# Cross attention and gated FFN on one core: loads placed in the list of steps, a new order of the steps, and a new order of the last products

## The chip, the cores and the metric

The kernel runs on one NeuronCore of a Trainium2 chip. What counts is the device time of one execution in microseconds (us); the figure given for a kernel is the median of its runs. The engines are TensorE (PE, its weight loads PEld), VectorE (DVE), ScalarE (ACT), GpSimd (POOL) and SyncE (SP); SP, ACT and POOL can issue DMAs.

## What is computed

There are 64 heads (8 batches b, 8 heads h) with 512 tokens x and 32 state rows each, of width 64. Tokens attend to the state rows, and state rows to the tokens, each without further projections. All 8 heads of a row are put side by side (width 512), and the rows, 512 + 32 per batch or 4352 in all, go through a gated FFN of inner width 1536.

```python
scores = scale * x @ state.T            # [512, 32] per head
xread  = softmax(scores) @ state        # tokens read the states
sread  = softmax(scores.T) @ x          # states read the tokens
rows   = concat([xread, sread], axis=2) # per batch 544 rows of 8*64
out    = (relu(rows @ w_gate) * (rows @ w_val)) @ w_out
```

## The kernel before, in words

**Attention and the first two FFN products in one.** As `xread` is a product with `state`, the kernel multiplies `state` with the weights first: U[b] = state[b] @ [w_gate, w_val] (steps `c` and `u`, line 299: many small matmuls, 64 rows by 32 columns; `co` and `uo` copy the result out of PSUM). A batch then needs, for each of 12 groups jf of 128 inner columns, four matmuls of 512 tokens (`ga` and `gb`, line 324): U's columns times the normalized scores of the batch, transposed (ANS). `re` (ScalarE, line 351) takes the relu of the gate half, `mu` (VectorE, line 355) the product with the value half; the result is h.

**How a batch gets its ANS.** `xT` transposes x on TensorE (line 169), `xo` copies it out, `sc` makes the scores (line 186), `ex` the exponent (ScalarE), `nr` the sums and their reciprocals (VectorE, lines 196 and 198), `nx` the scaling (line 202; VectorE, or GpSimd with `.pool`), `aT` the transpose (line 218), `ao` the copy. Each stands twice per batch, for four heads each. From batch 3 on, DMA transposes take the place of the TensorE ones.

**Down projection.** h @ w_out is made as seven products of half-size blocks, p1 to p7, instead of eight (`oh`, line 419). It needs sums of blocks: of h (`hs`, lines 385 to 387, and `hl`, line 394, on GpSimd) and of w_out (`ws.0` to `ws.3`, line 363, on GpSimd). `oc`, `oa` and `os` copy, add and store the four result blocks. The 256 state rows of all batches come last, as a ninth, smaller batch (`gvs`, line 342; `s_step`, lines 500 to 507).

**Order.** All is laid out by hand: the instructions of an engine run in the order in which they are written. For batches 0 to 2 and part of 3 the string `program` (lines 568 to 602) gives that order, word by word: `spin.7` is seven matmuls on zeros, `xT.1.0` a call of x_T(1, 0), and so on. Behind it a loop (line 650) goes through the remaining groups at a fixed lag of 18 groups between a group and its down projection. Last, `h_sums(B)` and a list of steps (line 663) run the rest: the products of the state rows, in the order p1, p2, p6, p5, p7, p4, p3, among those of the last batch (the zeros).

**Loads.** x of batch 0 comes in three parts: heads 0 and 1 over ACT's queue, heads 2 and 3 over SP's behind the states of batches 0 and 1 (lines 525 to 527), and heads 4 to 7 over GpSimd's queue, which converts to bf16 on the way. Before the first word of `program`, GpSimd issues every other load of the first stage in one go (lines 535 to 543): two pairs of 256 columns of w_gate and w_val, x of batch 1 in two halves, four more pairs, x of batch 2, the states of batches 2 to 7, and w_out in two halves. `c.b.i` needs pair i; `stT.0.2` needs the first states. The states of batches 0 and 1 come as fp32 and are cast by `stc`.

**The last stores.** The state rows' result is kept in one tile of two row blocks t of 128 rows (four batches) by two column halves m of 256. When a row block is complete (after p4, and after p3), four DMAs of 32 rows by 512 columns store it (lines 495 to 498).

Of the kernel before, what the change touches and what calls it, by code (L numbers as in the profile page):

```python
# [16 lines left out]
def kernel(  # L17
# [91 lines left out]
    def x_dma_cast(b, parts=1):

        cast_on_load.add(b)
        xb_alloc(b)
        v = xb[b].rearrange("p (h c d) -> p h c d", h=H, c=NC)
        for i in range(parts):
# [1 line left out]
            nc.gpsimd.dma_start(out=v[:, hs], in_=x[b, hs].rearrange("h (p c) d -> p h c d", c=NC))
# [289 lines left out]
    def o_half(b, n):  # L406

        p, c = PRODUCTS[n // 2], n % 2
        a, w = {"p1": (h_block(b, 0, 0), b11), "p2": (h_block(b, 1, 0), b21), "p3": (h_block(b, 1, 0), b22),
                "p4": (h_block(b, 1, 1), t4), "p7": (h_block(b, 0, 1), b12),  # L410
                "p5": (held.get(("s", b, 1)), t1), "p6": (held.get(("s", b, 2)), t2w)}[p]
# [6 lines left out]
        for i in range(HF):
            nc.tensor.matmul(ps[:, HM * c:HM * c + HM], a[:, i, 128 * c:128 * c + 128], w[:, i],  # L419
                             start=(i == 0 and (p in ("p1", "p2", "p5") and c == 0 or p == "p5" and b == B - 1)),  # L420
                             stop=(i == HF - 1),
                             skip_group_check=True)
# [60 lines left out]
    def s_end(p):  # L483

        outr = out.rearrange("(b s) m -> b s m", s=SP)
        if p == "p1":
# [4 lines left out]
        if p in ("p1", "p6", "p7", "p4"):
            nc.scalar.copy(out=dst, in_=held["acc", B, "w", 0][:, 0:HM])
        else:
            nc.vector.tensor_tensor(out=dst, in0=held["acc", B, "z", 0][:, 0:HM], in1=dst, op=ALU.add)
        if p in ("p4", "p3"):
            for bq in range(4):
# [1 line left out]
                eng.dma_start(out=outr[t * 4 + bq, S:SP], in_=held["sr"][bq * Ns:(bq + 1) * Ns, t])
# [12 lines left out]
    nc.vector.memset(warm, 0.0)
# [64 lines left out]
    re.0.5 c.0.3 mu.0.5 ga.0.4 gb.0.4 aT.1.0 co.0.3.1.act c.1.3 ao.1.0.dve re.0.4 co.0.3.0.act co.1.3.1.act
    mu.0.4 c.0.4 ga.0.6 gb.0.6 co.0.4.1.act ga.0.7 gb.0.7 co.0.4.0.dve co.1.3.0.act nx.1.1 ga.0.9 re.0.6
    re.0.7 aT.1.1 ao.1.1.act mu.0.6 mu.0.7 gb.0.9 re.0.9 ga.0.8 gb.0.8 re.0.8 mu.0.9 mu.0.8 ga.1.0 ga.1.1
    gb.1.0 ga.1.6 re.1.0 mu.1.0 gb.1.1 gb.1.6 ga.1.3 gb.1.3 ga.1.2 stT.2.4 re.1.1 re.1.6 re.1.3 mu.1.1
    sto.2.4.0.act gb.1.2 re.1.2 ga.1.5 gb.1.5 ga.1.4 gb.1.4 ga.1.7 mu.1.3 mu.1.6 mu.1.2 hs.0.0 re.1.5 mu.1.5  # L580
    gb.1.7 re.1.7 re.1.4 oh.0.0 mu.1.7 xT.2.0 xT.2.2 c.0.5 sto.2.4.1.act xT.2.1 mu.1.4 xT.2.3 co.0.5.1.dve
    xo.2.2.dve c.1.5 xo.2.1.dve co.1.5.1.dve xo.2.0.act co.0.5.0.act co.1.5.0.act ga.0.11 gb.0.11 re.0.11
    mu.0.11 xo.2.3.act ga.0.10 gb.0.10 sc.2.0 re.0.10 mu.0.10 hs.0.1 ga.1.10 gb.1.10 ex.2.0 re.1.10 ws.0.pool
    ga.1.11 sc.2.1 ex.2.1 u.2.1.0 gb.1.11 nr.2.0 re.1.11 oh.0.1 nx.2.0 uo.2.1.0.0.act mu.1.11 aT.2.0 mu.1.10
    c.1.4 uo.2.1.0.1.act u.2.0.0 ao.2.0.act oh.0.2 oh.0.3 co.1.4.0.dve ga.1.8 nr.2.1 xc.3.0.act ws.1.pool
    hs.0.2 oc.0.1 oh.0.4 co.1.4.1.act xc.3.1.pool uo.2.0.0.0.act nx.2.1.pool ga.1.9 xt.3 oa.0.3 oh.0.6
    ws.2.pool gb.1.8 re.1.8 gb.1.9 oh.0.5 ws.3.pool re.1.9 mu.1.8 aT.2.1 hl.0 uo.2.0.0.1.act xd.4 xc.4.0.pool
    xc.4.1.pool hs.1.0 ao.2.1.act oh.0.7 hs.1.2 ga.2.0 gb.2.0 mu.1.9 ga.2.3 gb.2.3 xt.4 hs.1.1 ga.2.1 gb.2.1
    re.2.0 oc.0.5 mu.2.0 re.2.1 ga.2.2 re.2.3 gb.2.2 re.2.2 mu.2.1 oh.0.8 xd.5 u.2.1.1024 mu.2.3 u.2.0.1024
    uo.2.0.1024.0.dve uo.2.1.1024.0.act uo.2.0.1024.1.act oh.0.9 u.2.1.512 u.2.0.512 oc.0.9 oh.0.10  # L590
    uo.2.0.512.0.act uo.2.1.512.1.act sc.3.0 uo.2.1.512.0.dve ga.2.5 oa.0.9 oh.0.12 oh.0.13 uo.2.1.1024.1.act
    ga.2.4 uo.2.0.512.1.act gb.2.4 oh.0.11 re.2.4 gb.2.5 ga.2.7 oc.0.11 oh.1.0 os.0.11 mu.2.2 ex.3.0 mu.2.4
    oa.0.13 re.2.5 sc.3.1 ga.2.6 mu.2.5 nr.3.0 gb.2.6 srm.0 nx.3.0 ex.3.1 oh.1.1 srn.0 re.2.6 gb.2.7 re.2.7
    mu.2.6 nr.3.1 ga.2.8 mu.2.7 gb.2.8 re.2.8 oh.1.2 mu.2.8 u.3.0.0 uo.3.0.0.0.act u.3.0.512 uo.3.0.512.0.act
    uo.3.0.0.1.act oh.1.3 stT.4.8 u.3.1.0 uo.3.1.0.0.act nx.3.1.pool ga.2.9 aD.3 gb.2.9 sto.4.8.0.act oc.1.1
    oa.1.3 re.2.9 mu.2.9 srm.1 srn.1 sto.4.8.1.act uo.3.0.512.1.act oh.1.4 oh.1.5 oc.1.5 ga.2.10 gb.2.10
    ga.2.11 re.2.10 gb.2.11 mu.2.10 re.2.11 mu.2.11 xc.5.0.act oh.1.6 oh.1.7 u.3.1.512 u.3.1.1024 u.3.0.1024
    oh.1.8 hs.2.0 uo.3.1.0.1.dve ga.3.0 gb.3.0 uo.3.1.512.0.act uo.3.0.1024.0.act xc.5.1.pool sc.4.0 ga.3.1
    oh.1.9 hl.1 uo.3.1.1024.1.dve hs.2.1 uo.3.1.1024.0.act uo.3.1.512.1.act hs.2.2 ex.4.0 ga.3.3 gb.3.1 re.3.0
    ga.3.2 uo.3.0.1024.1.dve re.3.1 gb.3.2 mu.3.0 oc.1.9 oa.1.9 re.3.2 gb.3.3 oh.1.10 re.3.3 xt.5 mu.3.3 srm.2  # L600
# [95 lines left out]
```

## Time and profile before

| what | us |
|---|---|
| median of 3 runs | 223.88 (223.06 to 224.71) |
| the profiled execution | 224.17 |
| its span, first to last instruction or DMA | 222.1 |
| PE busy in the span | 213.4 |
| first matmul of the program that is not a spin, start | 4.98 |
| first product of the down projection, start | 35.84 |
| last matmul, start of its group of six | 217.00 |
| last store, issue | 218.45 |

In a row of the timeline stand the start, the length, the engine, the line, the operation with its tiles (out<-in) and shapes, the number of instructions taken together, and, in brackets, how long the engine stood idle before and what ended that. In a row of windows stand, behind the stretch and its length, the busy time and number of instructions of PE, PEld, DVE, ACT and POOL, the granted clock, the share of the DMA engines and GB/s. In the groups of instructions stand the busy time, the mean of one in ns, and the idle time before them. In the DMA issues stand the size and the time from issue to landing, and in the queues' rows packets, MB and share.

### The profile page before, as it was taken

What the parts mean: (1) busy time and instruction counts of PE and PEld (TensorE: products, weight loads), DVE (VectorE), ACT (ScalarE), POOL (GpSimd) and SP (SyncE); (2) the same over time, 40 slices, a digit from 0 to 9 for tenths busy, and PEclk for the clock granted to TensorE, in tenths of its full rate; (3) what the DMA queues carried; (4) which work ended last, traced back from release to release, by engine and by line L of the source; (5) the groups of instructions that cost most, each with busy time, mean ns of one, the idle gap of its engine ahead of it and who ended that gap; (6) DMA issues with size and microseconds to landing.
All of it is one profiled execution on the core that took longest, in us unless ns stands there. A gap on an engine that the chain in (4) does not pass through costs nothing.

```text
span 222.1 us, 5525 instructions
## 1 busy us (share of the span) xinstructions
PE 213.4 (96%) x2214; PEld 139.3 (63%) x2214; DVE 150.3 (68%) x263; ACT 128.7 (58%) x247; POOL 164.1 (74%) x162
## 2 busy tenths in 40 slices
PE   6879999999999999999999999999999999999992
PEld 2535445565665657656765666566656666888881
DVE  3579967855486848878787778777977485343531
ACT  2468976876757883566556655656565454322231
POOL 7946199899999996699949993996299719933210
PEclk9999999999999999999999999999999999999998
DMA  6999999039195409920298037102320121021106
GB/s 160 193 196 196 193 201 282 20 62 265 31 206 201 97 0 207 243 72 3 74 233 218 3 91 191 52 0 97 83 61 0 50 97 47 3 96 47 50 27 209
DMA packets 42361, 25.32 MB, mean 114 GB/s; under 512 B 18816, under 2 KB 41856, under 8 KB 42336
## 3 DMA queue, kind: packets, MB, share of 16 engines
q1 hardware_dynamic: 29408, 17.04, 29.4%
q0 software_dynamic: 12416, 7.41, 22.1%
q10 hardware_dynamic: 512, 0.52, 0.7%
q8 instruction: 17, 0.28, 0.5%
q14 instruction: 8, 0.07, 0.1%
HBM read 18.35 MB, written 8.91 MB: 123 GB/s over the span
## 4 chain that ended last, share of the span: by engine, by line
PE 82%; POOL 7%; ACT 4%; DVE 3%; DMA 2%; issue 1%; DVEq 0%; POOLq 0%
PE gv_ps L324 34%; PE w_ps L419 17%; PE z_ps L419 12%; PE gv_ps L342 5%; PE up L299 4%; PE sc_ps L186 2%; DMA st_f<-in_state_dram 2%; POOL s L386 2%; POOL s L385 2%; POOL h_sb L387 2%; POOL h_sb L394 2%; PE zs_ps L419 1%; ACT g_sb L351 1%; PE ws_ps L419 1%; PE xT_ps L169 1%; PE upc L299 1%
## 5 line engine op out<-in xcount | busy, mean ns | idle before, releaser
L355 DVE TENSOR_TENSOR h_sb<-gv_ps,g_sb 128x512 bf16<-128x512 f32 (+1 forms) x108 | 69.1, 657 | 42.3 <-ACT g_sb L351 31.3
L324 PE MATMUL gv_ps<-ans,U 128*128 128x512 bf16 x384 | 94.9, 379 | 0.2
L351 ACT ACTIVATE g_sb<-gv_ps 128x512 bf16<-128x512 f32 (+1 forms) x108 | 61.4, 576 | 37.3 <-PE gv_ps L324 27.5
L419 PEld LDWEIGHTS <-h_sb 128*128 128x128 bf16 x510 | 49.4, 98 | 16.4 <-issue 1.7
L324 PEld LDWEIGHTS <-U 128*128 128x128 bf16 x384 | 35.7, 98 | 31.7 <-issue 1.7
L385 POOL TENSOR_TENSOR s<-h_sb 128x512 bf16<-128x512 bf16 x24 | 27.7, 1153 | 19.3 <-DVE h_sb L355 19.3
L394 POOL TENSOR_TENSOR h_sb<-h_sb,s 128x512 bf16<-128x512 bf16 x24 | 27.0, 1152 | 7.2 <-PE z_ps L419 7.2
L429 ACT COPY o_sb<-w_ps 128x512 f32<-128x512 f32 x32 | 18.8, 587 | 18.4 <-PE w_ps L419 15.8
L386 POOL TENSOR_TENSOR s<-s,h_sb 128x512 bf16<-128x512 bf16 x24 | 28.0, 1167 | 1.9
L309 ACT CAST U<-up 128x512 bf16<-128x512 f32 x43 | 22.7, 595 | 10.0 <-PE up L299 10.0
L387 POOL TENSOR_TENSOR h_sb<-h_sb 128x512 bf16<-128x512 bf16 x24 | 28.1, 1171 | 0.0
L419 PE MATMUL w_ps<-wo_sb,h_sb 128*128 128x256 bf16 x192 | 26.2, 273 | 0.0
L419 PE MATMUL z_ps<-wo_sb,h_sb 128*128 128x256 bf16 x186 | 24.1, 273 | 0.0
L419 PEld LDWEIGHTS <-s 128*128 128x128 bf16 x204 | 19.2, 98 | 7.7 <-issue 2.8
L435 DVE TENSOR_TENSOR o_sb<-z_ps,o_sb 128x512 f32<-128x512 f32 (+1 forms) x23 | 15.5, 675 | 6.8 <-ACT o_sb L429 4.2
L309 DVE CAST U<-up 128x512 bf16<-128x512 f32 x29 | 18.4, 684 | 1.6 <-PE up L299 1.6
L196 DVE TENSOR_REDUCE cs<-e_sn 128x16 f32<-128x512 bf16 x16 | 10.9, 680 | 5.4 <-ACT e_sn L190 5.4
L190 ACT ACTIVATE e_sn<-sc_ps 128x512 bf16<-128x512 f32 x16 | 9.6, 600 | 6.5 <-PE sc_ps L186 6.5
L419 PE MATMUL w_ps<-t2w,s 128*128 128x256 bf16 x96 | 13.0, 273 | 0.0
L419 PE MATMUL w_ps<-t,h_sb 128*128 128x256 bf16 x96 | 12.3, 272 | 0.1
L419 PE MATMUL z_ps<-t,s 128*128 128x256 bf16 x90 | 12.0, 273 | 0.0
L299 PEld LDWEIGHTS <-stT 64*32 64x32 bf16 x480 | 6.1, 89 | 7.1 <-issue 4.6
(86 smaller groups left out, 228.5 us busy)
## 6 DMA issues: line engine op xcount, KB each, us to landing
out_dram<-o_sb SPq DMA_DIRECT2D x31, 256.0 KB, 2.7
xf<-in_x_dram SPq DMA_DIRECT2D x4, 1024.0 KB, 6.9
wg_sb<-in_moe_w_gate_dram POOLq DMA_DIRECT2D x6, 256.0 KB, 9.4
wv_sb<-in_moe_w_val_dram POOLq DMA_DIRECT2D x6, 256.0 KB, 9.8
wo_sb<-in_moe_w_out_dram POOLq DMA_DIRECT2D x2, 768.0 KB, 15.7
xf<-in_x_dram POOLq DMA_DIRECT2D x1, 1024.0 KB, 18.8
xb<-in_x_dram POOLq DMA_DIRECT2D x3, 256.0 KB, 7.0
xb<-in_x_dram POOLq DMA_DIRECT2D x1, 512.0 KB, 11.8
```

The costliest lines, as they stand in the source:

```text
L299: nc.tensor.matmul(dst[kc][q:q + 32], stT[r:r + 64, b, j, 32 * sl:32 * sl + 32], wsb[r:r + 64, j, lo:lo + n], start=True, stop=True)
L309: copy[eng](out=U[b][:, w, kc, lo:lo + 512], in_=held["u", b, w, lo][kc])
L324: nc.tensor.matmul(ps[w], U[b][:, w, kc, f0:f0 + 128], ANS[b][:, kc].rearrange("p c t -> p (c t)"), start=(kc == 0), stop=(kc == NK - 1))
L351: nc.scalar.activation(out=g_sb[:, 0:n], in_=ps[0][:, 0:n], func=AF.Relu)
L355: nc.vector.tensor_tensor(out=dst, in0=ps[1][:, 0:n], in1=held["g", b, jf][:, 0:n], op=ALU.mult)
L385: tt(out=s_block(b, 1, i), in0=a21, in1=a22, op=ALU.add)
L386: tt(out=s_block(b, 2, i), in0=s_block(b, 1, i), in1=a11, op=ALU.subtract)
L387: tt(out=a21, in0=a11, in1=a21, op=ALU.subtract)
L394: {"dve": nc.vector, "pool": nc.gpsimd}[eng].tensor_tensor(out=a12, in0=a12, in1=s_block(b, 2, i), op=ALU.subtract)
L419: nc.tensor.matmul(ps[:, HM * c:HM * c + HM], a[:, i, 128 * c:128 * c + 128], w[:, i], start=(i == 0 and (p in ("p1", "p2", "p5") and c == ...
L429: nc.scalar.copy(out=o_sb, in_=held["acc", b, "w", 0])
L435: nc.vector.tensor_tensor(out=o_sb[:, cols], in0=banks[c if isinstance(c, int) else 0][:, cols], in1=o_sb[:, cols], op=ALU.add)
```

## The change

1. The state load on SP is written ahead of x's first load, and a new memset of one element of x's buffer stands before both on VectorE; x's load of heads 0 and 1 (ACT's queue) writes over that element and so waits for the memset. The memset of `stT` comes after it.
2. GpSimd's 18 remaining loads become steps, `gd.1` to `gd.18`, in their old sequence but at places of the list: two before the first matmuls and on either side of the states' cast, two ahead of `nx.0.0`, ten behind it up to `gd.14`, `gd.15` ahead of `nx.1.1`, three behind it. `x_dma_cast` can load one half at a time for that.
3. The list is ordered anew. The cast of the states and the scalings nx.0.0 and nx.1.1 move to GpSimd, two of the four sums of w_out (ws.0, ws.3) to VectorE; some copies change between ScalarE and VectorE; three more spins are in it.
4. In the last list p4 and p3 of the state rows come at the very end. The last product, p3, is made in two column halves of 128, each with its own add.
5. Each 128 x 256 block of the state rows is stored with one DMA as soon as it is complete, after p2, c22, p4 and p3.

```diff
-    stc.0.2.dve spin.7 stT.0.2 sto.0.2.1.act spin.1 xh.0.dve spin.1 xT.0.0 sto.0.2.0.dve xh.1.act xT.0.1
-    xo.0.0.dve xT.0.3 xo.0.1.dve sc.0.0 spin.1 xo.0.3.dve ex.0.0 nr.0.0 nx.0.0 xT.0.2 xo.0.2.act sc.0.1 ex.0.1
-    spin.1 nr.0.1 c.0.0 co.0.0.1.act c.1.0 nx.0.1 spin.1 xg.3 aT.0.0 aT.0.1 ao.0.0.dve co.0.0.0.act ga.0.0
-    c.1.1 co.1.0.1.dve c.0.1 co.1.0.0.act ao.0.1.dve gb.0.0 co.0.1.0.act co.0.1.1.dve ga.0.2 gb.0.2
...
+    gd.1 stc.0.2.pool xh.0.dve spin.7 gd.2 spin.1 xh.1.act stT.0.2 sto.0.2.0.act spin.1 spin.1 xT.0.0 xT.0.1
+    xo.0.1.dve xT.0.3 xo.0.3.dve spin.1 xo.0.0.act sto.0.2.1.act gd.3 gd.4 sc.0.0 ex.0.0 nr.0.0 xT.0.2
+    xo.0.2.act sc.0.1 spin.1 nx.0.0.pool spin.1 ex.0.1 c.0.0 gd.5 nr.0.1 nx.0.1 c.1.0 co.0.0.0.act spin.1
+    co.0.0.1.act co.1.0.0.dve co.1.0.1.act aT.0.0 spin.1 aT.0.1 c.1.1 c.0.1 ao.0.0.dve ga.0.0 co.0.1.0.act
+    ao.0.1.dve gb.0.0 re.0.0 ga.0.2 co.0.1.1.dve gb.0.2 re.0.2 co.1.1.0.dve ga.0.1 mu.0.0 gd.6 gd.7 gd.8 gd.9
+    gd.10 gd.11 gd.12 co.1.1.1.act ga.0.3 gb.0.3 re.0.3 gb.0.1 re.0.1 xT.1.0 xo.1.0.act mu.0.2 mu.0.1 xT.1.2
+    xo.1.2.act xT.1.3 xT.1.1 c.0.2 xo.1.1.act co.0.2.0.act c.1.2 sc.1.0 gd.13 mu.0.3 gd.14 xo.1.3.dve sc.1.1
+    co.0.2.1.dve ex.1.0 ga.0.5 co.1.2.1.act co.1.2.0.dve gb.0.5 re.0.5 gd.15 c.0.3 nr.1.0 nx.1.0 ga.0.4 gb.0.4
+    mu.0.5 ex.1.1 co.0.3.1.act nr.1.1 nx.1.1.pool re.0.4 co.0.3.0.act c.1.3 co.1.3.0.act aT.1.0 ga.0.6 c.0.4
...
+        parts = 2 if b == B and p == "p3" else 1
+        for q in range(parts):
+            lo, hi = HM * q // parts, HM * (q + 1) // parts
+            for i in range(HF):
+                nc.tensor.matmul(ps[:, HM * c + lo:HM * c + hi], a[:, i, 128 * c:128 * c + 128], w[:, i, lo:hi],
...
-        if p in ("p4", "p3"):
-            for bq in range(4):
-                eng = nc.sync if bq % 2 == 0 else nc.gpsimd if p == "p4" else nc.scalar
-                eng.dma_start(out=outr[t * 4 + bq, S:SP], in_=held["sr"][bq * Ns:(bq + 1) * Ns, t])
+            parts = 2 if p == "p3" else 1
+            for q in range(parts):
+                s = slice(HM * q // parts, HM * (q + 1) // parts)
+                nc.vector.tensor_tensor(out=dst[:, s], in0=held["acc", B, "z", 0][:, s], in1=dst[:, s], op=ALU.add)
+        if p in ("p2", "c22", "p4", "p3"):
+            eng = nc.scalar if p in ("p4", "c22") else nc.sync
+            eng.dma_start(out=outr[4 * t:4 * t + 4, S:SP, HM * m:HM * m + HM], in_=dst)
...
-    nc.vector.memset(stT, 0.0)
...
+    nc.vector.memset(xf[0][:, 0:1, 0:1, 0:1], 0.0)
+    nc.vector.memset(stT, 0.0)
+    state_dma(nc.sync, st_f, 0, 2)
     x0_dma(nc.scalar, xf[0], 0, 2)
-    state_dma(nc.sync, st_f, 0, 2)
     x0_dma(nc.sync, xf[0], 2, 4)
...
+    loads = []
     for i in range(6):
-        for s, d in ws:
-            w_dma(s, d, 256 * i, 256 * i + 256)
+        loads += [lambda s=s, d=d, i=i: w_dma(s, d, 256 * i, 256 * i + 256) for s, d in ws]
         if i == 1:
-            x_dma_cast(1, 2)
-    x_dma_cast(2)
-    state_dma(nc.gpsimd, st_b, 2, B)
-    wo_dma(0, 6)
-    wo_dma(6, NF)
+            loads += [lambda i=i: x_dma_cast(1, 2, (i,)) for i in range(2)]
+    loads += [lambda: x_dma_cast(2), lambda: state_dma(nc.gpsimd, st_b, 2, B), lambda: wo_dma(0, 6),
+              lambda: wo_dma(6, NF)]
...
-    for p in (0, "p1", "p2", "p6", 0, "p5", "p7", 0, "p4", 0, "p3", 0, 0, 0):
+    for p in (0, "p1", "p2", "p6", 0, 0, "p5", "p7", 0, 0, 0, 0, "p4", "p3"):
```

The rest of the list, up to its last word, is ordered anew in the same way.

More of the change, by code (lines that the diff above doesn't have):

```diff
@@ L107, with x_dma_cast @@
     cast_on_load = set()
[L109 to L114, printed above, removed]
+    def x_dma_cast(b, parts=1, which=None):
+        if b not in cast_on_load:
+            cast_on_load.add(b)
+            xb_alloc(b)
+            xb[b] = xb[b].rearrange("p (h c d) -> p c h d", h=H, c=NC)
+        for i in which or range(parts):
             hs = slice(H * i // parts, H * (i + 1) // parts)
-            nc.gpsimd.dma_start(out=v[:, hs], in_=x[b, hs].rearrange("h (p c) d -> p h c d", c=NC))
-        xb[b] = xb[b].rearrange("p (h c d) -> p c h d", h=H, c=NC)
+            nc.gpsimd.dma_start(out=xb[b].rearrange("p c h d -> p h c d")[:, hs],
+                                in_=x[b, hs].rearrange("h (p c) d -> p h c d", c=NC))
     def w_dma(src, dst, lo, hi):
@@ L417, in o_half @@
         ps = acc(b, which, c)
[L418 to L422, printed above, removed]
+        parts = 2 if b == B and p == "p3" else 1
[3 more added lines that the diff above has]
+                nc.tensor.matmul(ps[:, HM * c + lo:HM * c + hi], a[:, i, 128 * c:128 * c + 128], w[:, i, lo:hi],
+                                 start=(i == 0 and (p in ("p1", "p2", "p5") and c == 0 or p == "p5" and b == B - 1)),
+                                 stop=(i == HF - 1),
+                                 skip_group_check=True)
     def o_rows(b, t):
@@ L576 @@
[L576 to L600, printed above, removed]
@@ new lines @@
+    co.0.4.0.act ao.1.0.dve gb.0.6 ga.0.7 gb.0.7 re.0.6 mu.0.4 co.0.4.1.dve ga.0.9 ga.0.8 aT.1.1 gb.0.9 mu.0.6
+    gb.0.8 co.1.3.1.act ga.1.0 ao.1.1.dve gb.1.0 re.0.7 re.0.9 gd.16 gd.17 gd.18 mu.0.7 re.0.8 ga.1.6 ga.1.1
+    gb.1.1 gb.1.6 ga.1.3 gb.1.3 ga.1.2 gb.1.2 mu.0.9 re.1.0 re.1.1 re.1.6 re.1.3 ga.1.5 gb.1.5 mu.0.8 mu.1.0
+    mu.1.1 ga.1.7 xg.3 re.1.2 re.1.5 gb.1.7 re.1.7 mu.1.6 mu.1.2 mu.1.3 mu.1.5 ga.1.4 gb.1.4 re.1.4 xT.2.0
+    stT.2.4 sto.2.4.0.act xT.2.2 c.0.5 co.0.5.1.act mu.1.7 oh.0.0 xT.2.3 xT.2.1 hs.0.0 hs.0.1 c.1.5
@@ new lines @@
+    ga.2.4 gb.2.4 oh.0.13 re.2.4 oh.0.11 gb.2.5 ga.2.7 mu.2.2 oc.0.11 oh.1.0 os.0.11 mu.2.4 sc.3.1 oa.0.13
+    re.2.5 ga.2.6 gb.2.6 mu.2.5 srm.0 nr.3.0 nx.3.0 srn.0 uo.2.1.1024.1.act re.2.6 oh.1.1 ex.3.1 gb.2.7 re.2.7
+    mu.2.6 oc.1.1 nr.3.1 mu.2.7 ga.2.8 gb.2.8 re.2.8 oh.1.2 u.3.0.0 uo.3.0.0.1.act uo.3.0.0.0.act u.3.0.512
+    uo.3.0.512.1.act uo.3.0.512.0.dve mu.2.8 oh.1.3 stT.4.8 u.3.1.0 nx.3.1.pool sto.4.8.0.act aD.3 ga.2.9
+    gb.2.9 re.2.9 uo.3.1.0.0.act mu.2.9 srm.1 oh.1.4 oh.1.5 oa.1.3 oc.1.5 srn.1 ga.2.10 gb.2.10 re.2.10
@@ new lines @@
+    ga.2.11 sto.4.8.1.dve gb.2.11 re.2.11 mu.2.10 xc.5.0.act mu.2.11 oh.1.6 oh.1.7 u.3.1.512 u.3.1.1024
+    u.3.0.1024 oh.1.8 oh.1.9 uo.3.1.0.1.dve xc.5.1.pool hl.1 sc.4.0 uo.3.0.1024.0.act ga.3.0 gb.3.0 hs.2.0
+    hs.2.1 uo.3.1.1024.0.act uo.3.0.1024.1.dve uo.3.1.512.1.dve uo.3.1.1024.1.dve re.3.0 ex.4.0 hs.2.2
+    uo.3.1.512.0.dve ga.3.2 ga.3.1 gb.3.1 re.3.1 gb.3.2 ga.3.3 mu.3.0 oc.1.9 oa.1.9 re.3.2 srm.2 gb.3.3
+    oh.1.10 oh.1.11 re.3.3 xt.5 mu.3.1 oc.1.11 os.1.11 mu.3.3 srn.2 nr.4.0 nx.4.0.pool xd.6 mu.3.2
```

20 lines of the change are left out of this document (13 added, 7 removed).

## The prediction

> **What bounds the kernel now.** I read the page's first two parts, then one-microsecond windows, then the timeline of the first 45 us, the DMA issues one by one, and the tail of the timeline.
>
> ```profile
> PE 213.4 (96%) x2214; PEld 139.3 (63%) x2214; DVE 150.3 (68%) x263; ACT 128.7 (58%) x247; POOL 164.1 (74%) x162
> PE   6879999999999999999999999999999999999992
> DMA  6999999039195409920298037102320121021106
> ```
> TensorE is busy in every slice but the first four and the last one; the DMA engines are full in the first seven. So there are two places to win: the head, up to about 25 us, and the tail after the last matmul.
>
> ```profile
> 12.00:13.00 1.00, 0.00 (x0) 0.00 (x0) 0.93 (x4) 0.85 (x2) 0.74 (x1) 1.00 1.45 195
> ```
> Between 12 and 13 us no matmul starts, while the loads come at 195 GB/s: 256 KB in 1.34 us. The head, as it runs now (start, length, engine, line):
>
> ```profile
> 1.19 3.17 PE L554 MATMUL warm_ps<-warm 128*128 128x512 bf16 x7 [1.19 <-DVE warm L511]
> 1.27 0.93 POOL L520 DMA_DIRECT2D xb<-in_x_dram  x1 [0.83 <-POOLq L680]
> 4.45 0.48 DVE L129 CAST st_b<-st_f 128x256 bf16<-128x256 f32 x1 [2.24 <-DMA st_f<-in_state_dram]
> 6.27 1.50 POOL L116 DMA_DIRECT2D xb<-in_x_dram  x2
> 7.93 0.72 PE L186 MATMUL sc_ps<-stT,xT 128*128 128x64 bf16 x8
> 8.69 0.60 ACT L190 ACTIVATE e_sn<-sc_ps 128x512 bf16<-128x512 f32 x1 [1.98 <-PE sc_ps L186]
> 9.32 0.69 DVE L196 TENSOR_REDUCE cs<-e_sn 128x16 f32<-128x512 bf16 x1 [0.85 <-ACT e_sn L190]
> 10.04 0.25 DVE L198 RECIPROCAL rc<-cs 128x16 f32<-128x16 f32 x1
> 12.33 0.69 DVE L202 TENSOR_TENSOR a_sn<-e_sn,rc 128x512 bf16<-128x512 bf16 x1
> 13.08 0.40 PE L218 MATMUL aT_ps<-id,a_sn 128*128 128x128 bf16 x4 [1.10 <-DVE a_sn L202]
> 18.04 1.08 PE L169 MATMUL xT_ps<-id,xb 128*64 128x128 bf16 x32
> 23.45 0.29 PE L299 MATMUL upc<-wg_sb,stT 64*32 64x256 bf16 x4
> 23.95 0.29 PE L299 MATMUL upc<-wg_sb,stT 64*32 64x256 bf16 x4 [0.21 <-ACT g_sb L351]
> 24.43 0.30 PE L299 MATMUL upc<-wg_sb,stT 64*32 64x256 bf16 x8
> 24.54 0.30 PE L299 MATMUL upc<-wv_sb,stT 64*32 64x256 bf16 x8
> 24.78 2.36 PE L324 MATMUL gv_ps<-ans,U 128*128 128x512 bf16 x10
> 27.20 5.34 PE L324 MATMUL gv_ps<-ans,U 128*128 128x512 bf16 x24
> 35.84 0.82 PE L419 MATMUL w_ps<-wo_sb,h_sb 128*128 128x256 bf16 x6
> ```
> The chain is state, x, scores, exponent, sums, scaling, transpose. From 27.20 on, 24 matmuls take 5.34 us, 0.22 each: nothing waits any more, and whatever stands before is what an order can change.
>
> **The change, part by part.** *The load queue.* Today GpSimd issues all loads one behind the other (x1's two halves at 6.27 to 7.77) and only the DMA engines limit them. In the new list the fifth and all later loads stand behind nx.0.0, now on GpSimd, and that waits for the sums of the first scores.
>
> ```profile
> xb<-in_x_dram POOLq DMA_DIRECT2D x1, 256.0 KB, 7.0
> wv_sb<-in_moe_w_val_dram POOLq DMA_DIRECT2D x1, 256.0 KB, 9.2
> wv_sb<-in_moe_w_val_dram POOLq DMA_DIRECT2D x1, 256.0 KB, 10.4
> wv_sb<-in_moe_w_val_dram POOLq DMA_DIRECT2D x1, 256.0 KB, 10.9
> wo_sb<-in_moe_w_out_dram POOLq DMA_DIRECT2D x1, 768.0 KB, 14.5
> q0 software_dynamic: 22, 0.01, 27.4%
> q0 software_dynamic: 12, 0.05, 11.0%
> ```
> These are the single issues at 6.27, 8.46, 9.93, 12.19 and 19.30 with their time to landing, so they land at 13.3, 17.7, 20.3, 23.1 and 33.8. The two queue rows are of 4.0 to 4.3 us and of 215.06 to 217.0: GpSimd's first load, issued at 1.27, has its first packets at 4.0 to 4.3, and its store of 215.06 (its row stands with the tail's) between 216.7 and 217.0 (up to 216.7 the view has no row of this queue). So an issue into an empty queue shows packets 1.6 to 3.0 us later.
>
> ```profile
> L202 POOL TENSOR_TENSOR a_sn<-e_sn,rc 128x512 bf16<-128x512 bf16 x3 | 3.1, 1044 | 2.1 <-ACT g_sb L351 2.1
> ```
> When does nx.0.0 run? The scores: state lands at 4.4 as now (a few tenths earlier with x behind it). Its cast goes to GpSimd (on VectorE it took 0.48; I take some 0.5) and lies behind load 1 and ahead of loads 2 to 4, which go out 0.7 later than now, while the queue is full: nothing. x's ACT load waits for the new memset and goes out 0.5 us later (1.25, not 0.73); hidden, since the eight spins (0.43 each) and the two after the state's transposes hold TensorE to about 6.0. Then ScalarE has xh.1, three copies and sto in a row (0.6, 0.4, 0.6, 0.4), which puts sc.0.0 at 7.9, where it stands now. So the sums end at 10.3 again (10.04 + 0.25), the scaling takes 1.04, and load 5 goes out at 11.3 instead of 6.27. The four loads ahead run out at about 11.2. With 1.6 to 3.0 us to the first packets, 1.34 of data and 0.8 to the landing, x1's first half lands at 15.0 to 16.4 instead of 13.3: all loads from the fifth on are 1.7 to 3.1 us late. I take 2.3, the middle: one end is the program's very first load, the other a small store.
>
> Who needs them? The second scaling no longer queues behind the first on VectorE, so aT.0.1 comes at about 12.5 (13.08 now), and the 16 matmuls of groups 0 to 3 end near 17.3, 0.7 before the 18.04 of today. Then c.0.2, c.0.3 and c.0.4 need the third, fourth and fifth pairs of weights, whose second members land at 20.0, 22.6 and 25.4 (17.7, 20.3, 23.1 plus 2.3): TensorE waits for each. c.0.4's second half is at 25.4, not 24.54: 0.86 late, less two matmuls of ga.0.6 that now stand ahead of it (0.43): +0.45. For a shift of 1.7 this is -0.15, for 3.1 +1.25; it breaks even at 1.9. Past this, wo's first half lands at 33.8 + 2.3 = 36.1, and oh.0.0 comes at 37 (35.84, plus what moves ahead of it): hidden. nx.1.1 on GpSimd holds loads 16 to 18 until about 24.7; the queue then still has 5 us of data: hidden.
>
> *Order.* The three added spins (0.22 to 0.43 each) lie in today's waits, the 1.10 before 13.08 above all: nothing, and up to 1.0 where the waits go. c.1.3 and c.0.4 are now apart. Two groups of eight small matmuls inside one run start 0.11 apart (24.43, 24.54), the step from the last group to the full-size matmul of 24.78 is 0.24: 0.13 more on the way out, about as much on the way in, so +0.3 for one more run. Two of wo's sums go to VectorE:
>
> ```profile
> L363 POOL TENSOR_TENSOR t<-wo_sb 128x1536 bf16<-128x1536 bf16 x1 | 3.1, 3084 | 0.0
> L385 DVE TENSOR_TENSOR s<-h_sb 128x768 bf16<-128x768 bf16 x1 | 0.6, 558 | 0.1
> ```
> That is 6.2 us off GpSimd and twice 1.1 (2 x 0.56) onto VectorE, which is idle a third of the time: nothing for TensorE, though it unburdens the queue that feeds p6. The other swaps between ACT and DVE balance; I take 0, with 0.5 either way.
>
> *The tail.*
>
> ```profile
> 213.54 0.82 PE L419 MATMUL ws_ps<-t,h_sb 128*128 128x256 bf16 x6
> 214.38 0.81 PE L419 MATMUL w_ps<-t,h_sb 128*128 128x256 bf16 x6
> 215.06 1.08 POOL L498 DMA_DIRECT2D out_dram<-sr_sb  x2 [8.16 <-ACT sr_sb L492]
> 217.85 0.42 DVE L466 TENSOR_TENSOR o_sb<-zs_ps,o_sb 128x256 f32<-128x256 f32 x1 [0.23 <-PE zs_ps L419]
> 217.97 0.39 SPq L439 DMA_DIRECT2D out_dram<-o_sb  x1
> 218.45 0.46 SPq L467 DMA_DIRECT2D out_dram<-o_sb  x1
> out_dram<-o_sb SPq DMA_DIRECT2D x1, 128.0 KB, 2.7
> out_dram<-o_sb SPq DMA_DIRECT2D x1, 256.0 KB, 2.1
> ```
> Six matmuls take 0.66 between starts, but 213.54 to 214.38 is 0.84: a wait of 0.18 for a copy. Two products now lie between: -0.18. The last store lands 2.7 us after its issue; one with the queues to itself, twice as large, at 199.40, took 2.1. With eight stores of 64 KB made four of 128 KB and block r4 sent long before, I take -0.4 for landing and -0.1 for SP's issue just ahead (217.97 to 218.36). The last product in two halves: if the first add may run beside the second half, the last add covers 128 columns instead of 256 (between 0.21 and 0.42, I take 0.28): -0.14; if it waits for the whole product, two of 0.28 replace one of 0.42: +0.14. I take 0. Weight loads double, about +0.04. Tail: -0.64 (-0.8 to -0.3).
>
> **Sum.** The profiled execution took 224.17 (span 222.1), 0.29 over the median of 223.88. 224.17 + 0.45 + 0.3 - 0.64 = 224.28; from the median, 223.88 + 0.11 = 224.0.
>
> **A page's rule against the rows.** By the rows a GpSimd issue needs 1.6 to 3.0 us to its first packets. The Trainium skill, "DMA: Bandwidth & Descriptors", section "Latency and other measured facts", gives about 1 us for the first byte on this path. By it the hole is 1.1 us, and the sum would be that of the second rival. The trace does not agree: both of its issues into an empty queue took longer.
>
> **The rivals.**
> 1. *The hole closes.* If load 5 goes out two microseconds sooner (scores earlier), no load is late; then groups 0 to 3 end 0.7 sooner, and the waits in c.1.3 and c.0.4 (32 small matmuls from 23.45 to 24.78, which at 0.11 for eight need some 0.5) go, another 0.8: -1.5, with the tail 223.88 - 1.5 + 0.3 - 0.64 = 222.0, and 221.5 if the switch and the middle give too. Against it: GpSimd's scaling cannot start before 9.5 with these durations.
> 2. *A short hole.* With a shift of 1.1 the weights land at 24.2, ahead of need, and half of the first rival's gain is had: 223.88 - 0.75 - 0.34 = 222.8.
> 3. *Slower: GpSimd's queue holds the loads longer.* From a shift of 1.9 on, each microsecond costs one. Load 5 at 13.5 instead of 11.3 (a late x, a scaling delayed on GpSimd, TensorE slow for longer) means a shift of 4.5, +2.6: 223.88 + 2.6 + 0.3 - 0.64 = 226.1, and wo's first half at 38.3 then holds oh.0.0 as well. For it: this queue has its first wait on another engine's late result, and ten later loads stand behind it. Against: everything ahead of the scaling lies within 0.5 us of today.
>
> **How the numbers follow.** One per cent (2.24 us) is about what a measurement of this kernel can tell from no change. Forecast 0.55, closed 0.14, short 0.12, slower 0.19. Faster by over 1% (under 221.6) needs the closed hole and a little more: 0.14. Slower by over 1% (over 226.1) is the third rival with its tail of late loads: 0.18. Within: 0.68. The forecast's own range is 223.2 to 225.1; with the rivals' ends it goes from 221.7 to 226.1. Predicted: 224.0.
>
> **What would show it.** In the windows from 11 to 15 us the DMA share falls from 1.45 for 1.6 to 3 us; if it doesn't, the hole is wrong. The scaling L202 on POOL starts at 10.3; the L299 rows of c.0.2 to c.0.4 idle on DMAs; the first L419 has no DMA ahead of it. The last store's landing is near 2.2. If the matmuls of the third group (24 in 5.34) start before 27, the head has won; a middle with gaps between 30 and 60 us would make the prediction wrong in a way that I have not priced.

## The result and the profile after

The changed kernel takes 226.94 us (median of 4 runs, 226.65 to 227.21) where the kernel before took 223.47 beside it (4 runs): a ratio of 1.0146, interval 1.0099 to 1.0192. It is slower by 3.5 us (2.2 to 4.3 by the interval), outside the range forecast. The kernel before had a median of 223.94 in the 23 runs of the next set, so some 3.0 is as likely. The profiled execution took 226.65, its span 224.7.

**The head.** Timeline of the changed kernel, GpSimd and TensorE, as read in the prediction:

```profile
4.05 0.41 POOL L130 CAST st_b<-st_f 128x256 bf16<-128x256 f32 x1
5.85 0.76 POOL L121 DMA_DIRECT2D wv_sb<-in_moe_w_val_dram  x1
9.16 1.05 POOL L203 TENSOR_TENSOR a_sn<-e_sn,rc 128x512 bf16<-128x512 bf16 x1 [2.55 <-DVE rc L199]
10.15 1.56 POOL L117 DMA_DIRECT2D xb<-in_x_dram  x2
...
10.26 0.30 PE L300 MATMUL upc<-wv_sb,stT 64*32 64x256 bf16 x8 [0.66 <-DMA wv_sb<-in_moe_w_val_dram]
13.02 0.30 PE L300 MATMUL upc<-wv_sb,stT 64*32 64x256 bf16 x8 [1.01 <-DMA wv_sb<-in_moe_w_val_dram]
13.47 3.69 PE L325 MATMUL gv_ps<-ans,U 128*128 128x512 bf16 x15
17.09 1.08 PE L170 MATMUL xT_ps<-id,xb 128*64 128x128 bf16 x32
18.57 0.30 PE L300 MATMUL upc<-wg_sb,stT 64*32 64x256 bf16 x8 [0.41 <-DMA wg_sb<-in_moe_w_gate_dram]
19.91 0.30 PE L300 MATMUL upc<-wv_sb,stT 64*32 64x256 bf16 x8 [1.03 <-DMA wv_sb<-in_moe_w_val_dram]
22.59 0.30 PE L300 MATMUL upc<-wv_sb,stT 64*32 64x256 bf16 x8 [0.43 <-DMA wv_sb<-in_moe_w_val_dram]
25.93 0.30 PE L300 MATMUL upc<-wv_sb,stT 64*32 64x256 bf16 x8 [0.28 <-DMA wv_sb<-in_moe_w_val_dram]
28.64 7.93 PE L325 MATMUL gv_ps<-ans,U 128*128 128x512 bf16 x36
37.63 0.61 PE L423 MATMUL w_ps<-wo_sb,h_sb 128*128 128x256 bf16 x4
```

The scaling on GpSimd holds the fifth load until 10.15 (6.27 before), and from 18.57 on TensorE waits for a weight load at each pair. The waits before 10.26 and 13.02 are not of this kind: they are for loads 2 and 4, and load 4 was issued at 5.85, ahead of the scaling. Three windows of that stretch:

```profile
7.00:8.00 1.00, 0.71 (x16) 0.49 (x15) 0.03 (x1) 0.68 (x3) 0.00 (x0) 1.00 0.74 83
12.00:13.00 1.00, 0.01 (x2) 0.00 (x0) 0.56 (x2) 0.16 (x1) 1.00 (x2) 1.00 1.09 125
15.00:16.00 1.00, 1.00 (x6) 0.47 (x5) 0.83 (x2) 0.81 (x2) 1.00 (x2) 1.00 0.62 73
```

The issue of 10.15, x1's first half, with its time to landing:

```profile
xb<-in_x_dram POOLq DMA_DIRECT2D x1, 256.0 KB, 5.6
```

The DMA share, some 1.45 where the queue is full, drops to 1.09 and 0.62 behind the load that was held: the hole is there, in two pieces. The drop to 0.74 at 7 us is another thing: a later run, with eight loads issued ahead of the scaling, has 1.15 there and no drop at 12 and 15 us. But the hole is not where 3.5 us went. The first down product starts 1.8 us later (37.63 for 35.84), yet 16 of x's transposes and the 16 small matmuls of `c.0.5`, which ran behind it, now stand ahead, and the last group of products starts at 216.84, 0.16 sooner than the 217.00 of before.

**The tail.** The timeline of the changed kernel with TensorE's last product, VectorE's last adds and the last stores:

```profile
216.84 0.83 PE L423 MATMUL zs_ps<-wo_sb,h_sb 128*128 128x128 bf16 x12
216.94 0.44 SPq L471 DMA_DIRECT2D out_dram<-o_sb  x1
217.04 0.37 ACT L497 COPY sr_sb<-ws_ps 128x256 f32<-128x256 f32 x1 [0.58 <-PE ws_ps L423]
217.44 0.56 ACTq L505 DMA_DIRECT2D out_dram<-sr_sb  x1
217.71 0.49 DVE L502 TENSOR_TENSOR sr_sb<-zs_ps,sr_sb 128x128 f32<-128x128 f32 x2 [0.90 <-PE zs_ps L423]
218.22 0.55 SPq L505 DMA_DIRECT2D out_dram<-sr_sb  x1
```

The windows behind it:

```profile
219.00:220.00 1.00, 0.00 (x0) 0.00 (x0) 0.00 (x0) 0.00 (x0) 0.00 (x0) 0.90 0.25 40
220.00:221.00 1.00, 0.00 (x0) 0.00 (x0) 0.00 (x0) 0.00 (x0) 0.00 (x0) 0.50 0.24 71
221.00:222.00 1.00, 0.00 (x0) 0.00 (x0) 0.00 (x0) 0.00 (x0) 0.00 (x0) 0.50 0.27 87
222.00:223.00 1.00, 0.00 (x0) 0.00 (x0) 0.00 (x0) 0.00 (x0) 0.00 (x0) 0.50 0.19 66
```

The same stretch of the kernel before:

```profile
219.00:220.00 1.00, 0.00 (x0) 0.00 (x0) 0.00 (x0) 0.00 (x0) 0.00 (x0) 1.00 1.01 340
220.00:221.00 1.00, 0.00 (x0) 0.00 (x0) 0.00 (x0) 0.00 (x0) 0.00 (x0) 0.98 0.35 120
```

The last store is issued 0.23 sooner (218.22, not 218.45) and the span ends 2.6 later: 6.5 us behind that issue, not 3.65. In between the DMA engines are a quarter busy, at up to 87 GB/s where before it was 340: 0.25 is what 4 of 16 engines give. A block's store goes out as four batches of 32 rows of 1 KB, and four is the slowest (outermost) dimension of its destination. The first store of this form, after p2, lay under the products; a window of it in the changed kernel:

```profile
213.00:214.00 1.00, 1.00 (x11) 0.89 (x10) 0.76 (x2) 0.28 (x2) 0.00 (x0) 1.00 0.27 94
```

The Trainium skill, "DMA: Bandwidth & Descriptors", section "Why a DMA increments its semaphore by 16 and not by 1", says that a DMA takes the largest number of engines, at most 16, that divides the slowest dimension (other than 1) of both sides; the section "Rules for kernel authors" warns of an outermost dimension under 16. By it this store gets 4, a pair of batches 2. The traces agree: 0.25 here, 0.14 for pairs (below).

### The profile page after: what moved, and what is told of

Its sections match the earlier page's. It is cut to its first block, busy times and chain, and to the rows that moved or that the text cites. A ratio compares the mean times of both kernels' runs of the same rounds, so it can differ in the third digit from the quotient of the medians.

```text
span 224.7 us, 5513 instructions
## 1 busy us (share of the span) xinstructions
PE 209.4 (93%) x2194; PEld 138.1 (61%) x2223; DVE 153.4 (68%) x269; ACT 126.3 (56%) x242; POOL 160.4 (71%) x161
## 4 chain that ended last, share of the span: by engine, by line
PE 78%; POOL 10%; DMA 5%; ACT 2%; DVE 1%; issue 1%; DVEq 0%; POOLq 0%
PE gv_ps L325 30%; PE w_ps L423 17%; PE z_ps L423 12%; DMA wv_sb<-in_moe_w_val_dram 5%; PE gv_ps L343 5%; PE up L300 3%; PE warm_ps L560 2%; POOL s L387 2%; POOL s L386 2%; POOL h_sb L395 1%; POOL h_sb L388 1%; PE zs_ps L423 1%; PE sc_ps L187 1%; PE ws_ps L423 1%; POOL wg_sb L121 1%
## 5 line engine op out<-in xcount | busy, mean ns | idle before, releaser
L325 PE MATMUL gv_ps<-ans,U 128*128 128x512 bf16 x356 | 91.4, 379 | 1.8 <-ACT U L320 0.3
L310 ACT CAST U<-up 128x512 bf16<-128x512 f32 x39 | 20.7, 592 | 10.2 <-PE up L300 10.2
L423 PE MATMUL w_ps<-wo_sb,h_sb 128*128 128x256 bf16 x192 | 25.9, 273 | 0.0
L310 DVE CAST U<-up 128x512 bf16<-128x512 f32 x33 | 20.9, 682 | 2.0 <-PE up L300 2.0
L203 POOL TENSOR_TENSOR a_sn<-e_sn,rc 128x512 bf16<-128x512 bf16 x5 | 5.2, 1046 | 10.1 <-ACT U L320 5.1
```

Source lines behind the costliest of these rows:

```text
L310: copy[eng](out=U[b][:, w, kc, lo:lo + 512], in_=held["u", b, w, lo][kc])
L325: nc.tensor.matmul(ps[w], U[b][:, w, kc, f0:f0 + 128], ANS[b][:, kc].rearrange("p c t -> p (c t)"), start=(kc == 0), stop=(kc == NK - 1))
L423: nc.tensor.matmul(ps[:, HM * c + lo:HM * c + hi], a[:, i, 128 * c:128 * c + 128], w[:, i, lo:hi], start=(i == 0 and (p in ("p1", "p2", "p ...
```

## The experiments

The theory: the four-engine store makes the whole loss, and the remaining terms are about as forecast. The rivals: the new order of the loads (part 2) makes it, or the new order of the last products does. "Parts" are those of the change; each ratio is to the kernel before, run beside it.

**Parts 4 and 5 alone**: the kernel before with the new last list, the halved p3 and the new stores.

```diff
-    for p in (0, "p1", "p2", "p6", 0, "p5", "p7", 0, "p4", 0, "p3", 0, 0, 0):
+    for p in (0, "p1", "p2", "p6", 0, 0, "p5", "p7", 0, 0, 0, 0, "p4", "p3"):
...
+            eng = nc.scalar if p in ("p4", "c22") else nc.sync
+            eng.dma_start(out=outr[4 * t:4 * t + 4, S:SP, HM * m:HM * m + HM], in_=dst)
```

> The kernel before with parts 4 and 5 of the change alone (order of the last products, halves of p3, one store per block). Theory A, the form of the stores: a block's store has four batches as its outermost dimension and runs on 4 of the 16 DMA engines, so it ends late; the whole loss is here: 226.0 to 226.7, span about 2.6 over before, last store issued near 218.2 and the span's end about 6.5 later, DMA share near 0.25 in the last microseconds. Rival B, the late loads of the head cost the time: 222.8 to 223.3, the tail's forecast gain alone.

226.73 us against 223.94, ratio 1.0126 (1.0107 to 1.0144): +2.8 us, at the upper end of theory A. The last store is issued at 218.02, the span ends at 224.6.

**Parts 1 to 3 alone**: the changed kernel with the lines of that diff undone.

```diff
-    for p in (0, "p1", "p2", "p6", 0, 0, "p5", "p7", 0, 0, 0, 0, "p4", "p3"):
+    for p in (0, "p1", "p2", "p6", 0, "p5", "p7", 0, "p4", 0, "p3", 0, 0, 0):
...
```

> The changed kernel with the tail of the kernel before (parts 1 to 3 alone). Theory A: 223.2 to 223.9, as the late loads (first half of x1 lands at 15.7) are made up for by the middle, where the matmuls of the two kernels start within 0.3 us of each other from 60 us on. Rival B: 226 or more.

224.50, ratio 1.0032 (1.0018 to 1.0046): +0.56, somewhat more than theory A had. The two add up to 3.35; measured together, 3.47 (2.2 to 4.3). So the tail makes most of the loss, 2.8 us of it, and the head the rest. The next five runs change the stores, two of them with the layout of the state rows.

**One store on 16 engines.** The rows are put with the state row n ahead of the batch in `br`, so that a store's slowest dimension is 32:

```diff
-    br = const.tile([128, NJ, B, Ns], BF16, name="br")
+    br = const.tile([128, NJ, 2, Ns, B // 2], BF16, name="br")
...
-            eng.dma_start(out=outr[4 * t:4 * t + 4, S:SP, HM * m:HM * m + HM], in_=dst)
+            eng.dma_start(out=outr[4 * t:4 * t + 4, S:SP, HM * m:HM * m + HM].rearrange("b n m -> n b m"), in_=dst)
...
```

> The changed kernel with the state rows kept in the order (row, batch) instead of (batch, row), so that each block is still one store of 128 rows of 1 KB to the same places, but with 32 rows outermost. Theory A: all 16 DMA engines take part, DMA share near 1 for a short time, the last store lands 2.1 to 2.4 after its issue instead of about 5.6, and the time is 223.0 to 223.7, 3 less than the changed kernel. Rival C, one large store of rows scattered over four batches is slow in itself: no change against 226.9.

224.45, ratio 1.0026 (1.0012 to 1.004): 2.5 us of the loss gone, not the 3 expected. The last store, issued at 219.06, lands 2.1 us later, and from 219 to 220 the DMA share is 0.66, more than four engines give. From the last matmul's modelled end to the span's end it is now 3.64 us (4.28 in the kernel before), a gain of 0.64. Part of what is left was new, a price of the new layout in the normalization, whose writes now have a stride of 8 bytes. That group of instructions (ns: least, median, most) in this kernel:

```profile
L283 DVE TENSOR_TENSOR br<-sr_ps,rr x16: 435/444/453, 66.8 to 180.8; 64x128 bf16<-64x128 f32 x16
```

And in the changed kernel:

```profile
L283 DVE TENSOR_TENSOR br<-sr_ps,rr x16: 282/288/295, 66.7 to 179.8; 64x128 bf16<-64x128 f32 x16
```

444 ns for 288, and the products behind batches 0 to 2 move by 0.25, 0.19 and 0.26 us. From the first group of `w_ps<-t,h_sb` to the last group it takes 160.04 us (57.64 to 217.68), in the changed kernel 159.33 (57.51 to 216.84): 0.71 in all.

**Fewer engines.** Each block is stored by two DMAs of two batches.

```diff
-            eng.dma_start(out=outr[4 * t:4 * t + 4, S:SP, HM * m:HM * m + HM], in_=dst)
+            for bq in range(2):
+                eng = nc.scalar if bq % 2 else nc.sync
+                eng.dma_start(out=outr[4 * t + 2 * bq:4 * t + 2 * bq + 2, S:SP, HM * m:HM * m + HM],
+                              in_=dst[64 * bq:64 * bq + 64])
```

> The changed kernel with each block stored as two DMAs of two batches (64 rows) each, one on SP's and one on ACT's queue. Theory A: two DMA engines for each, the same two for both, so 128 packets of 0.046 take 2.9 instead of 1.5, and 5.9 for the last two blocks together: DMA share near 0.125 and 228 to 230. Rival C, smaller stores on two queues are faster than a large one: under 226.

231.69, ratio 1.0355 (1.0335 to 1.0374), beyond even the 228 to 230 of theory A. Two windows of its tail:

```profile
224.00:225.00 1.00, 0.00 (x0) 0.00 (x0) 0.00 (x0) 0.00 (x0) 0.00 (x0) 0.50 0.14 48
226.00:227.00 1.00, 0.00 (x0) 0.00 (x0) 0.00 (x0) 0.00 (x0) 0.00 (x0) 0.50 0.14 48
```

Two of 16 engines (0.125), half the rate, although SP and ACT each have such stores under way: both seem to use the same two. Two smaller DMAs instead of one make it 4.7 us slower still (231.69 against 226.94), so a smaller store is not what helps; the time goes with the number of engines. The run with four DMAs per block (below) bears this out.

**The layout moved to the reader.** `br` as in the changed kernel, the n-ahead order made where line 343 reads it, with a stride of 64 bytes.

```diff
-                nc.tensor.matmul(ps[w][:, 0:nt], wsb[:, j, f0:f0 + 128], br[:, j].rearrange("p b n -> p (b n)"),
+                nc.tensor.matmul(ps[w][:, 0:nt], wsb[:, j, f0:f0 + 128], br[:, j].rearrange("p (t b) n -> p t n b", t=2),
```

> As the kernel with rows outermost, but the state rows' values are written in their old order and only read as (row, batch) by the matmuls of the FFN. Theory A (16 engines for the store) with the strided writes of the normalization (444 instead of 289 ns, twice per batch, which put the matmuls back by 0.25, 0.19 and 0.26 in batches 0 to 2) as what e3 lost: 223.6 to 224.0, about 0.7 under e3, if the strided read of 256 columns stays at 109 ns per matmul; 96 matmuls at 10 ns more would give 1 us back. Rival: the matmuls lost time in e3 for another reason, then 224.4 again.

262.46, ratio 1.1756 (1.1718 to 1.1795), far from both expectations. Four matmuls of line 343 in a row in this kernel's timeline:

```profile
191.60 1.90 PE L343 MATMUL gv_ps<-br,wv_sb 128*128 128x256 bf16 x4
```

The same four in the changed kernel:

```profile
190.42 0.60 PE L343 MATMUL gv_ps<-br,wv_sb 128*128 128x256 bf16 x4
```

The group's row gives 607 ns for one with the stride, 273 without. From start to start that is (1.90 - 0.607) / 3 = 0.43 us for (0.60 - 0.273) / 3 = 0.11, and 96 of them make 31 of the 38 us that the run lost on the one with 224.45. The rest goes with the granted clock, which is 1.00 in the window from 190 to 192 us and 0.50 from 244 to 248: there six matmuls of the down projection take 1.25 us from start to start (244.26 to 245.51), not 0.66. What brought the clock down was not tried. The run says nothing on the store.

**Four DMAs of 32 rows per block**, by turns on SP and ACT.

```diff
-            eng = nc.scalar if p in ("p4", "c22") else nc.sync
-            eng.dma_start(out=outr[4 * t:4 * t + 4, S:SP, HM * m:HM * m + HM], in_=dst)
+            for bq in range(4):
+                eng = nc.scalar if bq % 2 else nc.sync
+                eng.dma_start(out=outr[4 * t + bq, S:SP, HM * m:HM * m + HM], in_=dst[32 * bq:32 * bq + 32])
```

> The changed kernel with each block stored as four DMAs of 32 rows of one batch, SP and ACT by turns. Theory A: 32 rows outermost, so all 16 engines, and the time falls by 2.5 to 3 against the changed kernel, to 223.6 to 224.2; the four issues in a row cost some 0.5 at the end. Rival C (scattered rows or the write itself): no fall.

224.76, ratio 1.0053 (1.0032 to 1.0074), 0.6 above the expected range. All 16 engines again (the DMA share is 1.03 from 219 to 220), but eight issues follow on each other: four on SP from 218.31 take 2.48 us. The last one goes out near 220.5 and lands 1.5 us later. Issue time takes the place of transfer time.

**Only the last block in four**, the others with one store each as changed.

```diff
+            if p != "p3":
+                eng = nc.scalar if p in ("p4", "c22") else nc.sync
+                eng.dma_start(out=outr[4 * t:4 * t + 4, S:SP, HM * m:HM * m + HM], in_=dst)
+            else:
...
```

> The changed kernel with only the last block (p3) in four DMAs of 32 rows; p2, c22 and p4 stay one store on 4 engines. p4's store, issued 0.8 before, then ends last: its own 128 packets on four engines are 1.5 and it starts late by itself (the first store of this form had its first packets 1.2 after the issue). Theory A: the end lies some 3.8 to 4.5 after p4's issue at 217.4, so 222.5 to 223 in the span, 224.6 to 225.2 in time: about half of the loss was p3 sharing its four engines with p4. If it is 226 or more, p4's store alone makes the loss.

226.69, ratio 1.0135 (1.0112 to 1.0157): the gain that I expected is missing. p4's store, on four engines, is issued at 217.88, and the small ones of 218.66 and after land up to 3.8 us after their issue, where the same stores took 1.5 to 2.5 in the run before:

```profile
out_dram<-sr_sb ACTq DMA_DIRECT2D x2, 32.0 KB, 3.8
```

The small stores seem to wait behind its packets. One four-engine store near the end is thus enough for nearly the whole loss, as the last sentence of the expectation had it.

**The hole closed**: on top of the run with the strided read, loads 1 to 8 ahead of all else on GpSimd, the states' cast back on VectorE.

```diff
-    gd.1 stc.0.2.pool xh.0.dve spin.7 gd.2 spin.1 xh.1.act stT.0.2 sto.0.2.0.act spin.1 spin.1 xT.0.0 xT.0.1
+    gd.1 gd.2 gd.3 gd.4 gd.5 gd.6 gd.7 gd.8 stc.0.2.dve xh.0.dve spin.7 spin.1 xh.1.act stT.0.2 sto.0.2.0.act spin.1 spin.1 xT.0.0 xT.0.1
...
```

> As e5, with loads 1 to 8 issued in one go again, ahead of nx.0.0 on GpSimd, and the states' cast back on VectorE. My theory of the head: no hole in the load queue, x1's first half lands near 13.3 and the third to fifth value weights near 17.7, 20.3 and 23.1, the waits of c.0.1 to c.0.4 for DMAs go, and the time is 0.7 to 1.5 under e5. Rival: the waits for DMAs only hide those for copies of ScalarE and VectorE, and the time is that of e5 within 0.3.

260.26, 2.2 below the run that it stands on, more than expected. Both carry the slow matmuls; a pair further down is without them.

**Four runs with the order made in the last step that writes h.** The n-ahead order is made by VectorE's product with the value half, for the state rows only, 12 instructions in all. `br` stays, the store is the 16-engine one of above.

```diff
+        if b == B:
+            dst = dst.rearrange("p (t n b) -> p t b n", t=2, n=Ns)
+            val_half = val_half.rearrange("p (t b n) -> p t b n", t=2, n=Ns)
+            gate_half = gate_half.rearrange("p (t b n) -> p t b n", t=2, n=Ns)
...
```

The first is the kernel before with parts 4 and 5 and this:

> The kernel before with parts 4 and 5 of the change, and the state rows of h written n before b in their last step on VectorE (the product with the value half, 12 instructions a run), so that the blocks' columns stand as state row n outermost and one store of a block can name n first (32 times 4 rows), on all 16 engines. Theory (the four-engine store is the whole loss, and the tail's rest is worth what was forecast): the loss of 2.8 us of the tail alone is gone and -0.64 is left, 223.0 to 223.5 beside a before of 223.7 to 223.9; last store lands about 2.1 after its issue. Rival (the new order of the last products costs by itself): 224 or more.

223.39 against 224.04, ratio 0.9965 (0.9949 to 0.9981): -0.65. The issues of its blocks' stores on SP, with the time to landing:

```profile
out_dram<-sr_sb SPq DMA_DIRECT2D x2, 128.0 KB, 2.1
```

The last one goes out at 218.29 and is there at 220.4.

The second is the whole changed kernel with this:

> The changed kernel, whole, with the state rows of h written n before b as in the run before and one store of a block on 16 engines; nothing in the normalization's writes is changed, so the 0.84 us that the earlier trial lost there should not come. Theory: last group of matmuls at 216.8 to 217.1 as in the changed kernel, 3.6 from the last matmul's end to the span's end, 223.2 to 223.8, below the kernel before by up to 0.5. Rival (strided writes on VectorE slow the last groups as they slowed the normalization): the 12 products take 0.6 rather than 0.42 each and the time is 224.2 or more.

224.08, ratio 1.0008 (0.9988 to 1.0027). The store's loss is gone, but it is 0.3 over what I expected. The last group starts at 217.48, not 216.8. The strided products, 0.63 to 0.74 us now for 0.42, aren't the reason: from the first group of `w_ps<-t,h_sb` to the last group it takes 159.35 us (58.13 to 217.48), in the changed kernel 159.33. This execution was already late there; its head waited longer for the weights (the rows at 19.91 and 25.93 of the changed kernel show 1.03 and 0.28). Eight profiled executions with this head reach that group at 57.41 to 58.38, so the 216.8 was read from an early one. The same rows here:

```profile
20.32 0.30 PE L300 MATMUL upc<-wv_sb,stT 64*32 64x256 bf16 x8 [1.32 <-DMA wv_sb<-in_moe_w_val_dram]
26.55 0.30 PE L300 MATMUL upc<-wv_sb,stT 64*32 64x256 bf16 x8 [0.53 <-DMA wv_sb<-in_moe_w_val_dram]
```

The third has the hole closed, by the edit of the list shown above:

> The kernel of the run before, with loads 1 to 8 issued ahead of all else on GpSimd and the states' cast back on VectorE, so that nothing makes the loads wait in GpSimd's queue until the scaling. Theory (the hole in the loads costs about 0.4 us on TensorE, as the trial of the early loads on top of the slow matmuls showed with starts 0.4 earlier): 0.4 less than the run before, 222.8 to 223.4, below both kernels. Rival (a later wait takes it back, such as the one on GpSimd's sums seen at 46 us): no difference to the run before, 223.2 to 223.8.

222.46, ratio 0.9935 (0.9915 to 0.9954): 1.6 below the run before it, and their runs do not overlap (221.92 to 223.07 against 223.15 to 225.09). The expectation of 0.4 was a quarter of it. GpSimd and TensorE's first long run of matmuls in its timeline:

```profile
8.45 0.80 POOL L121 DMA_DIRECT2D wv_sb<-in_moe_w_val_dram  x1
9.50 1.05 POOL L203 TENSOR_TENSOR a_sn<-e_sn,rc 128x512 bf16<-128x512 bf16 x1 [0.24 <-DVE rc L199]
...
27.61 7.93 PE L325 MATMUL gv_ps<-ans,U 128*128 128x512 bf16 x36
```

One of its windows:

```profile
15.00:16.00 1.00, 1.00 (x6) 0.39 (x4) 0.79 (x3) 0.73 (x3) 0.48 (x1) 1.00 1.49 196
```

Eight loads are out before the scaling, which starts at 9.50 (9.16 in the changed kernel, 9.73 in the run before). The DMA share is 1.49 where it fell to 0.62 in the changed kernel and to 1.14 in the run before, and TensorE's 36 matmuls in a row start 1.03 sooner than in the changed kernel and 1.64 sooner than in the run before (29.25). What the cast's place does in this and what the loads' places do was not told apart.

The fourth is this kernel with the last product and its add in one piece of 256 columns:

```diff
-        parts = 2 if b == B and p == "p3" else 1
+        parts = 1
...
-            parts = 2 if p == "p3" else 1
+            parts = 1
```

> The kernel of the run before, with the last product and its add in one piece again (256 columns) instead of two halves of 128. In the changed kernel both half adds run after the whole product (0.49 together, a single add of 256 columns took 0.42). Theory (the halves only add an instruction): 0.05 to 0.15 less than the run before. Rival (the halves help, the first add running beside the product's second half): 0.1 more.

222.30, ratio 0.9929 (0.9909 to 0.9949), the lowest of all. Its runs overlap with those of the third (221.97 to 223.02 against 221.92 to 223.07), so the times don't show a difference; the traces show a small one. From the last group's start to the last store's issue it is 1.31 us here (215.81 to 217.12), 1.39 there (216.53 to 217.92): the halves cost 0.08.

## Why the prediction was wrong

- **The step that failed** is the store in the tail: "With eight stores of 64 KB made four of 128 KB and block r4 sent long before, I take -0.4 for landing". It took the price from a store with as many bytes or more (256 KB in 2.1 us) and did not ask by how many engines it moves. By 218.22 to 224.7 it is 6.5 us from issue to the end of the span, not 3.65: +2.8 in place of -0.4. The store behind that price, at 199.40 in the kernel before, had a DMA share of 0.70 and 238 GB/s from 200 to 201, nearly three times what four engines give, and I did not bound the other case; yet the diff names the four batches as the outermost dimension.
- **The rest of the tail was right in its sign and near in its size.** With 16 engines the landing is 2.1, as I took from the other store, and the tail alone is worth -0.65 (-0.4 to -1.1 by the interval; forecast -0.64). That the two agree to 0.01 is luck: the landing gave 0.6 (2.7 to 2.1) where I took 0.4, and the halves cost something. The wait of 0.18 is gone: the row at 213.56 of the changed kernel's timeline shows twelve matmuls in one piece.

```profile
213.56 1.47 PE L423 MATMUL w_ps<-t,h_sb 128*128 128x256 bf16 x12
```

- **The halves** (0 between -0.14 and +0.14): the first add waited for the whole product. Both start from 217.71, 0.49 for two where one took 0.42; with the second set of weight loads it is +0.08, by the last run.
- **The load queue was near in its times, partly by luck.** Load 5 went out at 10.15 (forecast 11.3; 10.5 to 11.0 in the other seven executions with this head), x1's first half landed at 15.7 (15.0 to 16.4), the value weights at 19.9, 22.6 and 25.9 (20.0, 22.6, 25.4), w_out's first half at 36.1 (36.1). Two errors cancel in this: the load went out 1.1 sooner, and from issue to landing it took 5.6, not 3.7 to 5.1. Loads 2 to 4, which I held for unchanged, stood ahead of it and landed at 10.2, 11.6 and 13.0 for 8.9, 10.6 and 11.9. TensorE waited 0.66 and 1.01 us for loads 2 and 4, which the prediction did not have. The cast on GpSimd isn't shown to be the reason: load 2 landed at 9.9 to 10.6 in the eight kernels that have it there, at 9.8 to 10.5 in the three with the new head and the cast on VectorE, at 8.9 to 9.6 in the three with the old head. Part 1 is a candidate (the state lands at 3.0 to 3.1, not 4.4, and x's first load goes out later); it was not tried alone, and the cause stays open.
- **Parts 1 to 3** were to cost 0.45 + 0.3 = 0.75. Alone they cost 0.56 (0.4 to 1.0 by the interval), on top of the tail with 16-engine stores 0.69 (224.08 less 223.39). The size fits, but the path was in part another: in the profiled execution aT.0.1 came at 11.38, not 12.5, and the waits for loads 2 and 4 came in.
- **The rivals.** The closed hole did not come in this change. Made by hand, on the tail with 16-engine stores, it gives 222.46 for 223.39: -0.93, where the rival had -1.5 + 0.3 = -1.2. So it was near in size, and 1.6 below the changed head, but not by its own account: the loads were still later than before (x1's first half landed at 14.4, for 13.3), and waits for weights remained. The short hole had no place: the value weights came 2.2 to 2.8 late, not 1.1. The third, loads held for longer, would have ended near the measured time (226.1), but by something that was not at work: load 5 went out sooner than forecast, and parts 1 to 3 alone cost 0.56.
- **The sum again**, with +2.8 in place of -0.4: 224.17 + 0.45 + 0.3 - 0.24 + 2.8 = 227.5 for the profiled execution, which took 226.65. Most of the difference lies ahead of the tail: the terms before the last group put it 0.57 later (0.45 + 0.3 - 0.18), and in this execution, whose head was an early one, it started 0.16 sooner. The range missed since the tail's ends (-0.8 to -0.3) came from stores on 16 engines alone.

## What to carry to other kernels

Before merging stores, read the outermost dimension of both sides of the merged one: here it was 4, the store ran at a quarter of the DMA engines, and near the end of the kernel that counted in full. Put a longer dimension outermost (here the 32 state rows), and make the needed order in an instruction that has slack (here 12 products on VectorE, which grew by half or more and cost no time on TensorE). And look at which loads stand behind a late compute step in the queue that issues them: here the loads ahead of that step, with the states' cast back on VectorE, were worth 1.6 us.
